# Splitting the last value output over two PSUM banks and two copying engines, with a new order of the segment

## The chip, the cores and the metric

The kernel runs on one core of one Trainium2 chip. The metric is device microseconds (us) of one execution.

## The reference, cut to what matters

Two branches over the same 2048 tokens of width 640 are mixed by a gate. Branch A (sliding-window attention) is untouched. Branch B is the one that changes: 64 segments in a row, each of 8 memory tokens and 32 new tokens, 32 heads of 192, and the memory of a segment is the output of the one before.

```
g = sigmoid((x * gate_w).sum(-1));  out = g * A(x) + (1 - g) * B(x)
# B:
for s in range(64):
    h = concat([mem, x[:, 32*s:32*s+32]])            # 40 tokens x 640
    q, k, v = h @ Wq, h @ Wk, h @ Wv                 # 32 heads x 192
    p = softmax(mask(q @ k.T * 192**-0.5))
    o = (p @ v) @ Wo                                 # 40 x 640
    mem = o[:, :8];  out += [o[:, 8:]]               # the next segment needs mem
```

## The kernel before

A segment is worked off in four groups of eight heads. For each group there are chunks of the projections (q, k, v: 20 matmuls each), turns of q and k (tq, tk), scores (s) with the softmax on VectorE and ScalarE, the turn of p, the value output (pv: 12 matmuls) and the output projection (o: six row tiles of Wo with ten matmuls each, all four groups added up in one PSUM bank). TensorE works in exactly the order of STEP; the other engines are list-scheduled around it.

The weights of branch B do not all fit beside each other. 21 tiles of a segment (11 of 384 KB, 10 of 320 KB) are streamed from HBM again in every segment, through a ring of five slots; STREAMED names them. A load is issued by SyncE when the tile five before it has been used up.

```
RING = 5
STEP = "q0 k0 v0 tk0 tq0 k1 q1 s0 tk1 tq1 q2 s1 tq2 k2 k3 p0 tk2 q3 pv0 v1 s2 p1 o0 tk3 tq3 pv1 v2 s3 p2 o1 pv2 v3 p3 o2 pv3 o3"
STREAMED = {"q": ((), (), (3, 4), (4,)), "k": ((4,), (3, 4), (4,), (4,)), "v": ((), (4,), (4,), (4,)),
            "o": ((1, 3, 5), (2, 5), (2, 5), (1, 3, 5))}
KEPT = {..., "hT": (1, [P, KT, SEG])}               # one buffer for the turned input
...
def values(s, g):                                    # L933, L938
    o = sc.buf("mm")                                 # one PSUM bank for the three blocks
    ... 12 matmuls, block b into columns 160*b ...
    sc.op("ACT", act(480), lambda: nc.scalar.copy(OT, o[:, 0:480]), reads=[o], writes=[OT])
...
def oproj(s, g):                                     # L957
    for c in range(6):                               # row tile c of the group
        for r in range(2):
            i, b = divmod(2 * c + r, 3)              # pair of heads i, block b of OT
            ... 5 matmuls with rhs = OT[:, b, i, :] ...
    if g == 3:
        sc.op("DVE", ..., copy(hT_next[:, :, 0:MEM], ps_o), after=[xl])     # L968: memory of the next segment
...
if chunks % 12 == 0:                                 # after v3
    hts[s + 1] = load_x(s + 1)                       # L745: x part of the next hT, by DMA
```

## Time and profile before

| | kernel before |
|---|---|
| time, median of the first three runs | 2259.32 us (2255.68 to 2266.35) |
| profiled run: span, granted TensorE clock | 2254.3 us, 0.980 |
| first copy of a memory into hT (start of the segments proper) | 567.9 us |
| one segment, mean of 62 | 26.20 us |

### The profile page before, as it was taken

Reading aid. Unit: us, or ns where it says so; the run is one execution under the profiler, and the core shown is the slowest. Engines: PE = TensorE matmul, PEld = TensorE weight load, DVE = VectorE, ACT = ScalarE, POOL = GpSimd, SP = SyncE. Lnnn points to the kernel's source line nnn. Section 1 sums busy time; section 2 is a strip of 40 time slices with the busy share of each in tenths; the row PEclk is TensorE's granted clock in tenths of the full one; section 3 lists DMA queues with packets and bytes.
Section 4 is the critical chain, followed back from the end, with each engine's and each line's share of the span. In section 5 each row is a group of like instructions: output and inputs, shape, how many; then the busy total and the mean of one; then the engine's idle time right before and its main releaser. Section 6 shows DMA issues by size and latency. Waiting matters only on the chain.

```text
span 2254.3 us, 112850 instructions
## 1 busy us (share of the span) xinstructions
PE 2056.8 (91%) x49093; PEld 1497.5 (66%) x49093; DVE 1124.8 (50%) x3942; ACT 1055.2 (47%) x2385; POOL 692.7 (31%) x1999
## 2 busy tenths in 40 slices
PE   7999999998899899999999999999999989999995
PEld 5777777885666666666666666666666666666663
DVE  6988885233444444444444444444444444444444
ACT  4888886223344444444444344444434434444443
POOL 5555554012222222222222222222222222222220
PEclk9999999999999999999999999999999999999996
DMA  3322211677899999999999899989989988999997
GB/s 123 97 74 87 82 46 64 242 276 242 290 311 312 305 300 313 305 313 323 302 312 307 296 305 317 316 296 322 317 294 311 311 290 298 305 312 318 314 314 238
DMA packets 263840, 591.69 MB, mean 262 GB/s; under 512 B 54696, under 2 KB 71344, under 8 KB 263344
## 3 DMA queue, kind: packets, MB, share of 16 engines
q1 hardware_dynamic: 240096, 537.19, 71.4%
q0 software_dynamic: 18976, 43.03, 5.6%
q8 instruction: 384, 6.29, 1.1%
q10 hardware_dynamic: 4272, 4.26, 0.6%
q14 instruction: 112, 0.92, 0.1%
HBM read 554.98 MB, written 36.97 MB: 263 GB/s over the span
## 4 chain that ended last, share of the span: by engine, by line
PE 71%; DMA 19%; ACT 4%; issue 3%; POOL 1%; DVE 1%; SPq 0%; ACTq 0%; DVEq 0%; POOLq 0%
DMA t_w<-w_packed 17%; PE ps_o L957 12%; PE ps_k L787 9%; PE ps_q L787 9%; PE ps_v L787 7%; PE ps_pv L933 4%; PE p_m L282 4%; PE p_s L327 4%; PE t_psum L596 4%; PE tr_q L802 2%; PE t_psum L619 2%; PE tr_k L802 2%; PE p_o L411 2%; PE S_ps L859 2%; ACT t_tok L792 1%
## 5 line engine op out<-in xcount | busy, mean ns | idle before, releaser
L787 PEld LDWEIGHTS <-b_hT 128*32 128x32 bf16 x15360 | 372.1, 97 | 272.4 <-issue 42.4
L957 PE MATMUL ps_o<-t_OT,w_o 128*128 128x40 bf16 x8960 | 328.9, 180 | 60.7 <-ACT t_OT L938 44.5
L957 PEld LDWEIGHTS <-w_o 128*128 128x128 bf16 x8960 | 281.0, 96 | 69.3 <-issue 56.3
L957 PE MATMUL ps_o<-t_OT,t_w 128*128 128x40 bf16 x6400 | 263.8, 180 | 27.4 <-DMA t_w<-w_packed 17.6
L357 DVE CUSTOM_DVE_ANT_0 a_junk<-p_s,a_mask 128x384 bf16<-128x384 f32 (+2 forms) x512 | 253.6, 529 | 42.3 <-PE p_st L327 29.8
L834 POOL COPY t_K<-t_xqk 128x64 bf16<-128x64 bf16 x256 | 60.6, 237 | 679.0 <-PE S_ps L859 675.0
L787 PE MATMUL ps_q<-w_q,b_hT 128*32 128x384 bf16 x4352 | 229.1, 334 | 23.7 <-DVE b_hT L968 22.9
L387 ACT ACTIVATE a_pt<-p_st 128x384 bf16<-128x384 f32 (+2 forms) x512 | 219.9, 474 | 41.7 <-PE p_st L327 34.2
L938 ACT CAST t_OT<-ps_pv 128x480 bf16<-128x480 f32 x256 | 143.2, 559 | 202.6 <-PE ps_pv L933 195.2
L957 PEld LDWEIGHTS <-t_w 128*128 128x128 bf16 x6400 | 206.7, 96 | 38.1 <-DMA t_w<-w_packed 28.1
L787 PE MATMUL ps_v<-w_v,b_hT 128*32 128x384 bf16 x4352 | 226.4, 329 | 1.8 <-issue 1.6
L869 DVE TENSOR_REDUCE sm_mx<-S_ps 128x4 f32<-128x160 f32 x256 | 82.6, 323 | 257.9 <-PE S_ps L859 257.8
L787 PE MATMUL ps_k<-w_k,b_hT 128*32 128x384 bf16 x3840 | 205.3, 332 | 0.0
L792 ACT CAST t_tok<-ps_q 128x384 bf16<-128x384 f32 x256 | 122.7, 479 | 147.1 <-PE ps_q L787 143.1
L825 DVE COPY t_K<-tr_k 128x256 bf16<-128x256 bf16 x256 | 75.2, 294 | 225.3 <-PE tr_k L802 221.4
L395 POOL TENSOR_SCALAR_AFFINE_SELECT a_pt<-a_pt 128x512 bf16<-128x512 bf16 x240 | 147.6, 637 | 125.5 <-ACT a_pt L387 124.5
L916 DVE TENSOR_TENSOR t_PTx<-PT_ps,mk_x 128x320 bf16<-128x320 f32 x256 | 124.6, 487 | 105.3 <-PE PT_ps L909 105.3
L792 ACT CAST t_vtok<-ps_v 128x384 bf16<-128x384 f32 x256 | 122.7, 479 | 112.8 <-PE ps_v L787 112.8
L811 ACT COPY b_QT<-tr_q 128x384 bf16<-128x384 bf16 x256 | 123.0, 480 | 105.5 <-PE tr_q L802 105.5
L792 ACT CAST t_tok<-ps_k 128x384 bf16<-128x384 f32 x256 | 122.7, 479 | 105.4 <-PE ps_k L787 105.3
L757 POOL DMA_DIRECT2D t_xqk<-xbqk x256 | 139.4, 545 | 86.7 <-POOL b_QT L815 38.8
L875 ACT ACTIVATE S_ps<-S_ps 128x160 f32<-128x160 f32 x256 | 74.4, 291 | 155.7 <-DVE S_ps L872 141.3
(151 smaller groups left out, 4100.7 us busy)
## 6 DMA issues: line engine op xcount, KB each, us to landing
t_w<-w_packed SPq DMA_DIRECT2D x714, 384.0 KB, 4.9
t_w<-w_packed SPq DMA_DIRECT2D x640, 320.0 KB, 4.6
t_xqk<-xbqk POOLq DMA_DIRECT2D x256, 48.0 KB, 4.4
xbqk<-t_ts POOLq DMA_DIRECT2D x12, 768.0 KB, 5.4
w_q<-in_B_Wq_dram SPq DMA_DIRECT2D x17, 384.0 KB, 4.8
w_v<-in_B_Wv_dram SPq DMA_DIRECT2D x17, 384.0 KB, 9.1
xbv<-t_ts POOLq DMA_DIRECT2D x16, 384.0 KB, 3.5
t_xv<-xbv POOLq DMA_DIRECT2D x64, 96.0 KB, 4.6
```

The costliest lines, as they stand in the source:

```text
L282: nc.tensor.matmul(view()[:, gg, :], lhsT=Wp[:, kt, 4 * g:4 * g + 4, :].rearrange("p h d -> p (h d)"), rhs=T(k["xT"])[:, kt, :], start=(kt ...
L327: nc.tensor.matmul(T(out)[:, i * P:(i + 1) * P], lhsT=b if keys_first else a, rhs=a if keys_first else b, start=True, stop=True, tile_posi ...
L357: sc.op("DVE", 135 + n / 0.96, lambda: nc.vector.tensor_tensor_reduce(out=T(junk)[:, 0:n], in0=T(s)[:, 0:n], in1=mask[:, NKB * P - n:], op ...
L387: sc.op("ACT", act_ns(n), lambda: nc.scalar.activation(out=T(pt)[:, h % 4, 0:n], in_=T(s)[:, 0:n], func=ACT.Exp), reads=[s], writes=[pt])
L395: nc.gpsimd.affine_select(out=v, in_=v, compare_op=op, fill=0.0, base=0, pattern=[[0, 4], [sign, P]], channel_multiplier=-sign)
L757: sc.op("DMA", 500, lambda: nc.gpsimd.dma_start(tile_of(qk)[:].rearrange("p i b t -> p (i b t)"), xbqk[g, :, s].rearrange("p i c -> p (i c ...
L787: nc.tensor.matmul(t[32 * j:32 * j + 32, 0:384], lhsT=tile_of(hT)[:, kt, :], rhs=w[:, j * 384:(j + 1) * 384], start=(kt == kts[0]), stop=( ...
L792: sc.op("ACT", act(384), lambda: nc.scalar.copy(tile_of(tok)[:], b["tile"][:, 0:384]), reads=[b], writes=[tok])
L811: nc.scalar.copy(dst, tq["tile"][:].rearrange("p b (j t) -> p b j t", t=SEG))
L916: nc.vector.tensor_tensor(out=tile_of(dst)[:], in0=PT["tile"][:, i, :, :].unsqueeze(2).to_broadcast([P, 2, 4, L]), in1=mk.unsqueeze(1).uns ...
L938: sc.op("ACT", act(480), lambda: nc.scalar.copy(tile_of(OT)[:].rearrange("p b j l -> p (b j l)"), o["tile"][:, 0:480]), reads=[o], writes= ...
L957: nc.tensor.matmul(t[:, dt * L:(dt + 1) * L], lhsT=w[:, r * D + dt * P:r * D + (dt + 1) * P], rhs=OT["tile"][:, b, i, :], start=(g == 0 an ...
```

## The change

The intent: at the end of a segment TensorE waits for one ScalarE copy of all three blocks of the last value output. With block 0 in a bank of its own, ScalarE can copy it while TensorE still computes blocks 1 and 2, VectorE copies these, and Wo's row tiles are ordered by block so that the first 20 matmuls of the projection need block 0 alone. The opening of the segment is reordered too, and the streamed tiles are distributed anew.

```diff
-            i, b = divmod(2 * c + r, 3)
+            b, i = divmod(2 * c + r, 4)             # rows of Wo by block; also where Wo is packed
-STEP = "q0 k0 v0 tk0 tq0 k1 q1 s0 tk1 tq1 q2 s1 tq2 k2 k3 p0 tk2 q3 pv0 v1 s2 p1 o0 tk3 tq3 pv1 v2 s3 p2 o1 pv2 v3 p3 o2 pv3 o3"
+STEP = "k0 q0 tk0 q1 tq0 k1 s0 tq1 tk1 k2 q2 s1 p0 tk2 q3 v0 tq2 k3 pv0 v1 s2 p1 o0 tq3 tk3 pv1 v2 s3 p2 o1 pv2 v3 p3 o2 pv3 o3"
-        o = sc.buf("mm")
+        o = [sc.buf("mm")]
+        o.append(sc.buf("mm") if g == 3 else o[0])
 ... (the matmuls in two parts: block 0, blocks 1 and 2)
-        sc.op("ACT", act(480), ... copy(OT, o[:, 0:480]))
+        sc.op("ACT", act(160), ... copy(OTa, o[0][:, 0:160]))
+        if g == 3:
+            sc.op("DVE", dve(320), ... copy(OTb, o[1][:, 160:480]))
+        else:
+            sc.op("ACT", act(320), ... copy(OTb, o[1][:, 160:480]))
 ... (oproj reads OTa for row tiles 0 and 1, OTb for the others)
-STREAMED = {"q": ((), (), (3, 4), (4,)), "k": ((4,), (3, 4), (4,), (4,)), "v": ((), (4,), (4,), (4,)),
-            "o": ((1, 3, 5), (2, 5), (2, 5), (1, 3, 5))}
+STREAMED = {"q": ((4,), (4,), (), (3, 4)), "k": ((), (4,), (3, 4), (4,)), "v": ((), (4,), (4,), (4,)),
+            "o": ((1, 3, 5), (1, 3, 5), (2, 5), (2, 5))}
```

More of the change, by code (lines that the diff above doesn't have):

```diff
@@ L713, in branch_B @@
         "tok": (2, [P, 384]), "vtok": (1, [P, 384]), "K02": (1, [P, 4, 2, L]),
-        "PTm": (1, [P, 2, 4, L]), "PTx": (1, [P, 2, 4, L]), "OT": (1, [P, 3, 4, L]), "Pm": (1, [P, 4, SEG]),
+        "PTm": (1, [P, 2, 4, L]), "PTx": (1, [P, 2, 4, L]), "OTa": (1, [P, 1, 4, L]), "OTb": (1, [P, 2, 4, L]), "Pm": (1, [P, 4, SEG]),
         "xqk": (2, [P, 2, 12, MEM]), "xv": (1, [P, 384]), "oT": (1, [P, KT, SEG]),
@@ L924, in values, with f @@
         V, xv = made.pop(("v", s, g)), tails[s]
-        o = sc.buf("mm")
-        def f():
-            t = tile_of(o, [P, 512], FP32, "ps_pv")
-            for b in range(3):
+        o = [sc.buf("mm")]
+        o.append(sc.buf("mm") if g == 3 else o[0])
+        def f(part):
+            t = tile_of(o[part], [P, 512], FP32, "ps_pv")
+            for b in (1, 2) if part else (0,):
                 for i, (p, v) in enumerate(((PTx, tile_of(xv)), (PTm, V["tile"]))):
@@ L933, in f @@
                         nc.tensor.matmul(t[64 * a:64 * a + 64, 160 * b:160 * b + 160], lhsT=v[:, c:c + 64],
-                                         rhs=p["tile"][:, a, :, :].rearrange("p j l -> p (j l)"), start=(b == 0 and i == 0),
+                                         rhs=p["tile"][:, a, :, :].rearrange("p j l -> p (j l)"), start=(i == 0 and (b == 0 or b == 1 and g == 3)),
                                          stop=(i == 1), tile_position=(0, 64 * a), skip_group_check=True)
-        sc.op("PE", 430, f, reads=[PTm, PTx, V, xv], writes=[o], name=("pv", s, g), mode=64)
-        OT = sc.buf("OT")
-        sc.op("ACT", act(480), lambda: nc.scalar.copy(tile_of(OT)[:].rearrange("p b j l -> p (b j l)"), o["tile"][:, 0:480]),
-              reads=[o], writes=[OT])
+        for part in range(2):
+            sc.op("PE", 143 * (1 + part), lambda part=part: f(part), reads=[PTm, PTx, V, xv], writes=[o[part]], name=("pv", s, g, part), mode=64)
+        OT = [sc.buf("OTa"), sc.buf("OTb")]
+        flat = lambda k: tile_of(OT[k])[:].rearrange("p b j l -> p (b j l)")
+        sc.op("ACT", act(160), lambda: nc.scalar.copy(flat(0), o[0]["tile"][:, 0:160]), reads=[o[0]], writes=[OT[0]])
+        if g == 3:
+            sc.op("DVE", dve(320), lambda: nc.vector.tensor_copy(flat(1), o[1]["tile"][:, 160:480]), reads=[o[1]], writes=[OT[1]])
+        else:
+            sc.op("ACT", act(320), lambda: nc.scalar.copy(flat(1), o[1]["tile"][:, 160:480]), reads=[o[1]], writes=[OT[1]])
         made["O", s, g] = OT
@@ L954, in f @@
             for r in range(2):
-                i, b = divmod(2 * c + r, 3)
+                b, i = divmod(2 * c + r, 4)
                 for dt in range(KT):
                     nc.tensor.matmul(t[:, dt * L:(dt + 1) * L], lhsT=w[:, r * D + dt * P:r * D + (dt + 1) * P],
-                                     rhs=OT["tile"][:, b, i, :], start=(g == 0 and c == 0 and r == 0 and dt == 0),
+                                     rhs=OT[b > 0]["tile"][:, b - (b > 0), i, :], start=(g == 0 and c == 0 and r == 0 and dt == 0),
                                      stop=(g == 3 and c == 5 and r == 1), skip_group_check=True)
         for c in range(6):
-            sc.op("PE", 10 * 25.4, lambda c=c: f(c), reads=[OT] + [wb[c]] * (wb[c] is not None), writes=[o_b], name=("o", s, g, c),
+            sc.op("PE", 10 * 25.4, lambda c=c: f(c), reads=[OT[c > 1]] + [wb[c]] * (wb[c] is not None), writes=[o_b], name=("o", s, g, c),
                   mode=128, after=[loads.get(("o", g, c))])
```

## The prediction

> **What bounds the kernel now.** I began with the slices of the page, to find the stage, then took the busy times of one stretch, then the waits of the matrix engine in it, then single rows of one segment.
>
> ```profile
> PE   7999999998899899999999999999999989999995
> DMA  3322211677899999999999899989989988999997
> ...
> 568.00:2192.00 1624.00, 1487.71 (x39184) 1067.13 (x39184) 730.38 (x2542) 685.91 (x1550) 447.16 (x1426) 0.99 0.92 308
> ...
> PE ps_o L957 <- ACT t_OT L938: 43.8, 62, 0.7
> PE ps_q L787 <- DVE b_hT L968: 22.6, 62, 1.7
> PE ps_o L957 <- issue: 16.4, 22, 1.8
> PE ps_o L957 <- DMA t_w<-w_packed: 15.5, 40, 1.2
> PE tr_q L802 <- ACT t_tok L792: 12.7, 61, 0.2
> ...
> DVE b_hT L968 <- DMA b_hT<-xa_dram: 25.8, 6, 5.0
> ```
>
> The slices show two regimes. The first quarter (sliding-window branch and the projections of the tails) hardly feels this change. From slice 10 on, TensorE and the DMA engines are both at nine tenths: the memory branch, 64 segments in a row, each of which needs the output of the one before. The stretch from 568 to 2192 us (the long row: TensorE 1487.71 of 1624.00 us busy, DMA share 0.92, 308 GB/s) holds exactly 62 of them, so one segment takes 1624 / 62 = 26.2 us. The time follows from what happens within a segment, times 64.
>
> The waits say that TensorE stands still for the value output of the last head group (t_OT, 43.8 / 62 = 0.71 us a segment, every time), for the new memory (b_hT, 0.36), for a token copy (0.20), and for weights that are streamed from HBM. The next rows show the first of these in one segment:
>
> ```profile
> 1220.57 0.24 PE L933 MATMUL ps_pv<-t_PTm,t_vtok 128*64 128x160 bf16 x2
> 1221.51 0.40 PE L957 MATMUL ps_o<-t_OT,w_o 128*128 128x40 bf16 x10 [0.71 <-ACT t_OT L938]
> ...
> 1220.90 0.56 ACT L938 CAST t_OT<-ps_pv 128x480 bf16<-128x480 f32 x1 [2.37 <-PE ps_pv L933]
> 1223.44 0.29 ACT L971 CAST t_oT<-ps_o 128x160 bf16<-128x160 f32 x1 [1.98 <-DVE b_hT L968]
> ...
> 1218.26 0.54 POOL L745 DMA_DIRECT2D b_hT<-xa_dram  x1 [2.40 <-PE PT_ps L909]
> ...
> DMA to landing us min/median/max: 2.8/4.2/5.7
> ```
>
> The last value matmul starts at 1220.57, ScalarE starts its 480-column copy 0.33 us later and takes 0.56, and the output projection starts 0.04 after that: a serial chain in which TensorE has nothing else to do, since this is the end of the segment. The last two rows matter below: the x part of the next segment's hT is fetched when the last v chunk is done, and lands 4.2 us (median) after its issue.
>
> **What the Trainium skill says.** "PSUM — Partial Sum Buffer", section "PSUM bank collisions raise a hardware error", says that a reader must not touch a bank while TensorE writes it. That is why one bank forces the copy to wait for all three blocks, and why the change takes a second bank; the trace agrees as far as it goes (the copy always starts after the last value matmul). "Perfetto Trace Analysis", section "Optimizing Scalar/DVE Operations", advises to break up an instruction that causes bubbles elsewhere on an engine that is not saturated: ScalarE is busy 685.91 of 1624 us and VectorE 730.38, so both have room. "Runtime: NRT & Kernel Launch", section "Instruction fetch mechanics", says instructions come in blocks of 256 over a DMA queue of their own, the cost mostly hidden. The trace agrees on the size (instruction queue: 384 packets, 6.29 MB, so 16.4 KB each, and 2 x 49093 TensorE instructions make 64 bytes each) but not on "hidden": the waits marked "issue" at ps_o come at places a multiple of about 255 TensorE rows apart, up to 1.8 us long. "TensorEngine Tiling (Array Packing)", section "Key Properties", says that a change of tiling mode drains TensorE; here the step between the last matmul of one mode and the first of another is about 0.095 us longer than within a mode (for example 0.149 against 0.056 us from a transpose to a projection chunk).
>
> **The change part by part.** (1) *Two banks, two engines, in group 3.* Block 0 goes to one bank in four matmuls, blocks 1 and 2 to another in eight. ScalarE can start 0.33 us after the second pair of block 0 (1220.29 in the segment above), so at 1220.62; 160 columns take 0.29 us (the t_oT copy has this shape); the projection can start at 1220.62 + 0.29 + 0.04 = 1220.95 instead of 1221.51. Its first 20 matmuls read block 0 alone, since Wo's rows are now ordered by block, and take 20 x 0.025 = 0.50 us, to 1221.45. VectorE starts at 1220.90; I estimate 0.49 us for 320 columns from the 0.48 us of its 320-element PSUM operations, done at 1221.43. It is just in time, so the wait falls by 0.56 us a segment and about 0.15 to 0.2 stays.
>
> (2) *Groups 0 to 2* get two ScalarE copies (0.29 + about 0.43 us) instead of one of 0.56: 3 x 0.16 us more ScalarE a segment. Between value output and projection there lies a v chunk, 0.93 us or more, so nothing waits. Cost on the path: none.
>
> (3) *New order.* I walked through the opening by hand with the durations of the rows (chunk 0.815, scores 0.43, transposes 0.17). The wait of tr_q for the token copy goes, since p0, tk2, q3 and v0 now lie between q2 and tq2: with the lost overlap 0.27 us. But the order has 26 changes of tiling mode instead of 24: 2 x 0.095 = 0.19. The new close spots (tk0 one chunk after k0, s0 one chunk after tq0, p0 right after s1) come out with 0.02 to 0.2 us to spare. Net gain 0.08.
>
> (4) *Which weights are streamed.* As many as before: 11 of 384 KB and 10 of 320 KB a segment, 8.08 MB with the rest. The transfers are no faster, only placed elsewhere: o0 to o3 stream 3, 3, 2, 2 row tiles instead of 3, 2, 2, 3.
>
> PE-side sum: 0.56 + 0.08 = 0.64 us a segment, 64 x 0.64 = 41 us. I do not expect to get it all.
>
> **What takes the place of the wait.** *First, the weight stream.* The ring has five slots; a load is issued when the tile five before it is used up (0.03 to 0.3 us after, by the rows) and lands 4.2 to 5.3 us later on average, depending on the place. So a tile waits where five tiles are used in under about 4.9 us. I measured this span in every segment: the third tile of o0 has 4.43 us at the shortest and costs TensorE 0.21 us on average, the second 4.74 and 0.10, the last of o3 4.17 and 0.12, the last of k1 4.94 and 0.15. With the few others this is about 0.75 us a segment. Laying out the new order with the same durations, the spans in o0 and o3 get longer (5.0 us and more), but o1 gets about 4.6, 4.0, 4.0 and o2 4.1 and 3.7. To bring these up to the 4.5 that the others end at takes about 0.8 us, together about 1.1: 0.35 more than now. Some of it is not new, because the instruction block that stalls around o2 (about 0.4 us a segment of "issue") arrives meanwhile; I count 0.2. There is also the rate itself: 8.08 MB in 25.6 us is 316 GB/s against 308 now; the best single segment had 325 GB/s in 24.49 us, so the floor of the stream is near 24.9 us a segment.
>
> *Second, the load of hT.* For each segment I compared its landing with the end of the last ps_o matmul: in 6 of 62 it came later (the row of 25.8 us above), and in 31 the lead was under 0.5 us. Taking 0.55 us from the time between issue and end raises the mean lateness from 0.07 to 0.23 us: 0.16 is lost, some less if o2 waits for weights in the same interval; I count 0.1.
>
> Sum: 0.64 - 0.2 - 0.1 = 0.34 us a segment, 64 x 0.34 = 22 us; 2259 - 22 = 2237, rounded to 2238.
>
> **Rivals.** (a) *The gain comes through whole.* For it: the t_OT wait is there in all 62 segments and nothing hides it. Against it: DMA at 0.92. Time: 2259 - 41 = 2218. If the more even opening also removes weight waits, a little under 2214. (b) *The stream is the bound.* For it: nine tenths in every slice, and the tight spans in o1 and o2. Against it: loads are mostly issued late because the ring waits for TensorE, so there is some room in the engines. Time: 2250 to 2262, the old time. (c) *hT becomes the end of the segment.* Then the t_OT wait reappears as a longer b_hT wait; time 2245. (d) *A slip in the opening:* scores or p0 waiting in each segment, 0.3 us or more; time 2255 to 2270. My walk speaks against it, with little margin.
>
> **Range and chances.** Runs of one kernel spread by 10 us here, and rivals (a) and (b) bracket the rest: 2210 to 2264. For over 2% faster it must fall under 2214, which needs the full gain and something more: 0.11. Over 2% slower needs 0.7 us a segment of new waits, more than any rival gives: 0.03. Within 2%: 0.86.
>
> **What would show it.** Right: a ps_o wait for the block-0 copy of about 0.15 to 0.2 us a segment instead of 0.71, no wait of the third row tile for VectorE, tr_q's wait gone, t_w waits in o1 and o2 up, a larger share of DMA releases before b_hT. The prediction is wrong if the weight waits fall although the segment got shorter (then the places of the loads matter more than my spans say), or if S_ps or PT_ps shows a new wait.

## More of the kernel before

The slices and waits are read in the prediction. One view it does not show is the chain that ended last, followed back from the last instruction: first the shares of the span by engine, then by instruction group. This is the kernel before:

```profile
PE 71%; DMA 19%; ACT 4%; issue 3%; POOL 1%; DVE 1%; SPq 0%; ACTq 0%; DVEq 0%; POOLq 0%
DMA t_w<-w_packed 17%; PE ps_o L957 12%; PE ps_k L787 9%; PE ps_q L787 9%; PE ps_v L787 7%; PE ps_pv L933 4%; PE p_m L282 4%; PE p_s L327 4%; PE t_psum L596 4%; PE tr_q L802 2%; PE t_psum L619 2%; PE tr_k L802 2%; PE p_o L411 2%; PE S_ps L859 2%; ACT t_tok L792 1%
```

The largest single entry is already the stream of weights (t_w, 17%); the copy of the value output, which the change attacks, is inside "ACT 4%".

## The result, and the profile after

The changed kernel takes 2288.76 us (median of 4 runs, 2280.26 to 2297.33); the kernel before took 2260.49 in the same rounds (4 runs, 2255.68 to 2266.35). The ratio is 1.0124, with a 95% interval from 1.0075 to 1.0173. Ratios and intervals are from fast runs of the same rounds, so not quite the ratio of the medians quoted. The kernel became slower, by about 28 us, and the time lies outside the predicted range.

The slices of the changed kernel (TensorE and the DMA engines, busy tenths in 40 slices):

```profile
PE   7999999998899999999989999899999999999995
DMA  4322211768899999999999999999998999999898
```

The stretch of its 62 segments, 575 to 2218 us (columns: length, busy time and instruction count of TensorE, its weight loads, VectorE, ScalarE and GpSimd, then granted clock, DMA share, GB/s):

```profile
575.00:2218.00 1643.00, 1510.09 (x39184) 1064.83 (x39176) 768.19 (x2603) 676.48 (x1736) 447.13 (x1426) 0.99 0.92 305
```

The picture is the same, only 19 us longer: 1643 us instead of 1624 for the same 62 segments, so 26.5 instead of 26.2 us each, at 305 instead of 308 GB/s. The waits of TensorE in this stretch (columns: total us, times, longest):

```profile
PE ps_o L964 <- DMA t_w<-w_packed: 57.8, 95, 2.6
PE ps_k L787 <- DVE b_hT L975: 45.0, 62, 1.8
PE ps_o L964 <- ACT t_OTa L942: 9.9, 61, 0.2
PE ps_o L964 <- issue: 8.8, 16, 1.0
```

And two waits of VectorE in the same stretch:

```profile
DVE b_hT L975 <- DMA b_hT<-xa_dram: 94.8, 50, 2.8
DVE b_hT L975 <- PE ps_o L964: 16.6, 11, 3.4
```

The wait for the value output fell from 43.8 to 9.9 us, as intended, and tr_q no longer waits for a token copy. But the output projection now waits 57.8 us for streamed weights (15.5 before), and the first chunk of the next segment 45.0 us for hT (22.6 before). The two VectorE rows say why hT is late: in 50 of 61 segments its copy waits for the load of x (6 before).

Rows of one segment of the changed kernel (start, duration, engine, line, operation, count, idle time before and its releaser):

```profile
1227.96 0.40 PE L964 MATMUL ps_o<-t_OTb,w_o 128*128 128x40 bf16 x10
1229.05 0.42 PE L964 MATMUL ps_o<-t_OTb,t_w 128*128 128x40 bf16 x10 [0.69 <-DMA t_w<-w_packed]
...
1235.58 0.23 PE L935 MATMUL ps_pv<-t_PTm,t_vtok 128*64 128x160 bf16 x2
1235.98 0.66 PE L964 MATMUL ps_o<-t_OTa,w_o 128*128 128x40 bf16 x20 [0.16 <-ACT t_OTa L942]
...
1237.93 1.00 PE L787 MATMUL ps_k<-w_k,b_hT 128*32 128x384 bf16 x20 [0.29 <-DVE b_hT L975]
```

The last three rows are the split at work: from the last value matmul to the projection it takes 0.40 us here, where the rows of before had 0.94, and the remaining row tiles follow without a wait for VectorE. The first two rows are what went wrong, in o1: its third streamed tile is not there yet.

The chain that ended last, in the changed kernel:

```profile
PE 64%; DMA 22%; issue 8%; POOL 3%; ACT 2%; DVE 1%; SPq 0%; POOLq 0%; DVEq 0%; ACTq 0%
DMA b_hT<-xa_dram 10%; PE ps_q L787 10%; PE ps_k L787 10%; DMA t_w<-w_packed 9%; PE ps_v L787 6%; PE ps_o L964 5%; PE p_m L282 4%; PE p_s L327 4%; PE t_psum L596 4%; PE ps_pv L935 3%; PE tr_q L802 2%; PE tr_k L802 2%; PE S_ps L859 2%; PE S_ps L852 2%; PE p_o L411 2%
```

The load of hT's x part, which was not among the entries of before, now leads the list with 10%: where it is the last to arrive, the chain runs through it and not through the matmuls and weights beside it.

**Where the time went.** I summed the rows in two ways. First, TensorE's waits of over 0.15 us by what ended them, in us per segment (mean of 62 segments of the profiled run, from one hT copy to the next):

| per segment, us | value copy | token copy | weights | hT | issue | segment |
|---|---|---|---|---|---|---|
| before | 0.71 | 0.21 | 0.44 | 0.37 | 0.41 | 26.20 |
| changed | 0.16 | 0.01 | 0.96 | 0.73 | 0.23 | 26.51 |

The removed waits (0.55 and 0.20) came back as 0.52 for weights and 0.36 for hT, less 0.18 for issue: the waits together came out level (2.14 before, 2.09 after). What the segment is longer by is time in which TensorE counts as busy, 1510.09 instead of 1487.71 us for the same matmuls in the two stretches above, 0.36 us a segment. Of this, 0.19 are the two more changes of tiling mode that the prediction booked, and about 0.11 is an estimate for the clock (13.6 us more of half clock, at half speed); part of the wait in o1 is booked as busy, too (at full clock its matmuls count 1.84 instead of 1.62 us), while other groups got a little shorter.

Second, for the segments that ran wholly at full clock I took the shortest time that each of the 36 groups of TensorE work ever took, start to start, and summed them: that is the segment without accidents. It fell from 24.41 to 23.83 us, by 0.58. The mean above that rose from 1.53 to 2.30 us, by 0.77; 0.88 of the 2.30 lie in o1 and 0.59 in o3 with the start of the next segment. So at full clock a segment is 0.19 us longer, 62 x 0.19 = 12 us. The other 7 or 8 us of the 19.5 that the segments lost come from stretches at half clock: 44 us in 13 of them, against 31 us in 7 (not counting one of 10 us at the start of each). The rest of the 24.3 us between the profiled runs lies outside: 6.6 us ahead of the first hT copy (half of it in branch A, which is the same code and had more half-clock time in that run), less 1.7 us at the end.

### The profile page after: what moved, and what is told of

Read it like the earlier page. It is cut to its first block, busy times and chain, and to the rows that moved or that the text cites. A ratio compares the mean times of both kernels' runs of the same rounds, so it can differ in the third digit from the quotient of the medians.

```text
span 2278.6 us, 113297 instructions
## 1 busy us (share of the span) xinstructions
PE 2084.5 (91%) x49093; PEld 1497.6 (66%) x49093; DVE 1164.2 (51%) x4006; ACT 1045.4 (46%) x2577; POOL 692.5 (30%) x1999
## 4 chain that ended last, share of the span: by engine, by line
PE 64%; DMA 22%; issue 8%; POOL 3%; ACT 2%; DVE 1%; SPq 0%; POOLq 0%; DVEq 0%; ACTq 0%
DMA b_hT<-xa_dram 10%; PE ps_q L787 10%; PE ps_k L787 10%; DMA t_w<-w_packed 9%; PE ps_v L787 6%; PE ps_o L964 5%; PE p_m L282 4%; PE p_s L327 4%; PE t_psum L596 4%; PE ps_pv L935 3%; PE tr_q L802 2%; PE tr_k L802 2%; PE S_ps L859 2%; PE S_ps L852 2%; PE p_o L411 2%
## 5 line engine op out<-in xcount | busy, mean ns | idle before, releaser
L787 PEld LDWEIGHTS <-b_hT 128*32 128x32 bf16 x15360 | 364.5, 97 | 277.7 <-DVE b_hT L975 52.0
L964 PE MATMUL ps_o<-t_OTb,t_w 128*128 128x40 bf16 x5120 | 211.5, 180 | 66.8 <-DMA t_w<-w_packed 60.1
L787 PE MATMUL ps_k<-w_k,b_hT 128*32 128x384 bf16 x4096 | 219.2, 335 | 45.9 <-DVE b_hT L975 45.3
L787 PE MATMUL ps_q<-w_q,b_hT 128*32 128x384 bf16 x4096 | 218.6, 334 | 0.1
L964 PE MATMUL ps_o<-t_OTb,w_o 128*128 128x40 bf16 x5120 | 189.7, 179 | 5.4 <-issue 3.4
L964 PE MATMUL ps_o<-t_OTa,w_o 128*128 128x40 bf16 x3840 | 138.8, 180 | 12.0 <-ACT t_OTa L942 10.2
L327 PE MATMUL p_s<-a_k,a_q 64*128 64x128 bf16 x1440 | 146.6, 220 | 0.7 <-issue 0.7
L327 PE MATMUL p_st<-a_qa,a_k 64*128 64x128 bf16 x1440 | 143.2, 219 | 3.8 <-ACT a_pt L387 2.4
```

The lines of the kernel that those rows point to most:

```text
L327: nc.tensor.matmul(T(out)[:, i * P:(i + 1) * P], lhsT=b if keys_first else a, rhs=a if keys_first else b, start=True, stop=True, tile_posi ...
L787: nc.tensor.matmul(t[32 * j:32 * j + 32, 0:384], lhsT=tile_of(hT)[:, kt, :], rhs=w[:, j * 384:(j + 1) * 384], start=(kt == kts[0]), stop=( ...
L964: nc.tensor.matmul(t[:, dt * L:(dt + 1) * L], lhsT=w[:, r * D + dt * P:r * D + (dt + 1) * P], rhs=OT[b > 0]["tile"][:, b - (b > 0), i, :], ...
```

## The experiments

Theory A: the gain of the split is real, and it is lost because three streamed tiles in o1 come too close together (the wait for weights) and the load of hT has too little time (the wait for hT); undo both and the gain appears. Theory B: TensorE's waits are only where the DMA side shows; the segment runs at the pace at which streamed weights come, and what is removed in one place returns in another. Later a third suspect joined, the blocks of instructions that are fetched through the same DMA engines.

All results agreed with the reference, also those that use wrong weights (e5 to e8): the comparison is not tight enough to see a few of Wo's row tiles exchanged.

| run | median us | before, same rounds | ratio [95%] | us per segment |
|---|---|---|---|---|
| e1: changed, old plan for Wo | 2262.99 | 2265.40 | 0.9999 [0.9976, 1.0022] | 26.21 |
| e2: changed, two hT buffers | 2267.19 | 2265.40 | 1.0007 [0.9987, 1.0026] | 26.25 |
| e3: both | 2261.48 | 2265.40 | 0.9980 [0.9963, 0.9996] | 26.23 |
| e4: before with the split alone | 2260.67 | 2265.40 | 0.9983 [0.9929, 1.0036] | 26.09 |
| e5: before, three tiles less streamed | 2172.50 | 2259.12 | 0.9635 [0.9606, 0.9663] | 24.93 |
| e6: e3, three tiles less streamed | 2159.96 | 2259.12 | 0.9581 [0.9548, 0.9614] | 24.62 |
| e7: before, six slots | 2288.67 | 2259.12 | 1.0141 [1.0101, 1.0181] | 26.13 |
| e8: e1, six slots | 2286.68 | 2259.12 | 1.0134 [1.0103, 1.0164] | 26.03 |
| e9: before with new order and plan, no split | 2301.12 | 2265.29 | 1.0160 [1.0111, 1.0209] | 26.81 |
| e10: before, blocks pinned early | 2240.78 | 2265.29 | 0.9906 [0.9870, 0.9943] | 25.97 |
| e11: before, blocks pinned in o2 | 2283.94 | 2265.29 | 1.0085 [1.0053, 1.0117] | 26.51 |
| e12: e13 with pinned blocks | 2222.38 | 2265.29 | 0.9812 [0.9773, 0.9851] | 25.61 |
| e13: before with split and two hT | 2247.24 | 2262.68 | 0.9908 [0.9880, 0.9936] | 26.09 |
| e14: e3 with pinned blocks | 2249.84 | 2262.68 | 0.9961 [0.9937, 0.9984] | 26.07 |
| e15: changed, pinned blocks | 2282.81 | 2262.68 | 1.0080 [1.0053, 1.0107] | 26.55 |
| e16: e13 with another pinned place | 2224.72 | 2262.68 | 0.9814 [0.9769, 0.9859] | 25.67 |

The last column is from the profiled run of each kernel, 62 segments.

### First set: undo the parts (e1 to e4)

**e1**, the changed kernel with the distribution of Wo's streamed tiles of before (three in o3, two in o1):

```diff
-            "o": ((1, 3, 5), (1, 3, 5), (2, 5), (2, 5))}
+            "o": ((1, 3, 5), (2, 5), (2, 5), (1, 3, 5))}
```

> The changed kernel with one thing undone: the row tiles of Wo that are streamed in o0, o1, o2, o3 are 1,3,5 / 2,5 / 2,5 / 1,3,5 again, as before, instead of 1,3,5 / 1,3,5 / 2,5 / 2,5. New order, split value output and the new streaming of q and k stay. Theory A (the third streamed tile of o1 is used too soon after the tile five places before it, and costs 0.8 us a segment; the whole of o1 takes 2.57 us instead of 1.63): o1 falls back to about 1.65 us, some waits return in o3 (0.1 to 0.2 us), the wait of the first k chunk for hT falls a little or stays near 0.7 us; the segment shortens by 0.5 to 0.8 us, the whole by 30 to 50 us: 2240 to 2260. Theory B (the new order as such is at fault, through hT's late landing and the DMA rate of 308 GB/s): the weight waits only move to another place and the time stays within 10 us of the changed kernel's 2289.

**e2**, the changed kernel with two buffers for hT, so that the load of x need not wait until the segment's last v chunk has read the old one:

```diff
-"hT": (1, [P, KT, SEG])
+"hT": (2, [P, KT, SEG])
```

> The changed kernel with two hT buffers instead of one, so that the x part of the next segment is fetched a whole segment earlier, and the copy of the new memory never waits for its landing. Theory A (hT's landing costs 0.73 - 0.29 = 0.44 us a segment on the path, beside the waits in o1): b_hT waits fall to 0.29 us a segment, landing never ends the wait of L975, the weights' ring gets its slots a little sooner, and of 0.44 x 64 = 28 us about half to all comes through: 2262 to 2276. Theory B (the weight stream binds alone, and whatever is gained at hT is lost again at o1's third tile): under 8 us, 2281 or more, with o1 growing from 2.57 us by about as much as hT's wait falls.

**e3**, both edits.

> Both: the changed kernel with the old plan of Wo's streamed tiles and two hT buffers. Theory A (two separate losses hide a real gain of about 0.8 us a segment on the matrix engine's side): 2215 to 2235, faster than the kernel before by 1 to 2%; the segment at 25.3 to 25.6 us. Theory B (the stream's rate is the floor, whatever the order): not under 2250, DMA share above 0.93 in all stretches.

**e4**, the kernel before with the split and Wo's rows by block, but with the STEP and STREAMED of before.

> The kernel before with only the first part of the change: value output of the last group in two banks copied by two engines, Wo's row tiles ordered by block; old order, old streaming plan. Theory A: the wait of o3 for the value output falls from 0.71 to about 0.17 us a segment as it did in the changed kernel, but the b_hT wait rises from 0.36 to 0.6 or more because the landing does not move; a gain of 0.2 to 0.4 us a segment, 2235 to 2250. If the split itself is what hurts (extra instructions on ScalarE and VectorE, another PSUM buffer of three held), 2265 or more.

Measured: waits of TensorE in the 62 segments of e1:

```profile
PE ps_o L964 <- issue: 22.5, 33, 1.7
PE ps_k L787 <- DVE b_hT L975: 21.2, 62, 1.7
PE ps_o L964 <- DMA t_w<-w_packed: 18.7, 44, 1.7
```

The same of e2:

```profile
PE ps_o L964 <- DMA t_w<-w_packed: 62.1, 81, 2.8
PE ps_k L787 <- DVE b_hT L975: 18.1, 62, 0.3
```

e1 takes the 28 us back: ratio 0.9999 where the changed kernel had 1.0124. The wait for weights at ps_o falls from 57.8 to 18.7 us and, without hT being touched, its wait falls from 45.0 to 21.2: hT now lands after the last ps_o matmul in 5 segments instead of 51, because the third tile of o3 holds up the segment's end instead. e2 shows the mirror image. With hT ready early its wait shrinks to 18.1 us, never over 0.3 (that is the copy itself), the time is back at that of before (1.0007), and the wait for weights grows. So either remedy alone removes the loss. Both together (e3) are worth no more than one: 0.998. Theory A expected 2240 to 2260 us for e1 (missed by 3 us), 2262 to 2276 for e2 (met), 2215 to 2235 for e3 and 2235 to 2250 for e4; the last two missed, though e4's four runs split (two near 2249, two near 2272), so that its ratio is the least certain. In e4 the value copy's wait is 0.16 us a segment, and the weights' wait has risen from 0.44 to 0.61. In all four, 26.1 to 26.25 us per segment remain, as before the change. Theory B looks better.

### Second set: what sets the pace (e5 to e8)

**e5** leaves out three of the 21 streamed tiles, all of Wo (12% of a segment's bytes), and uses a neighbouring resident tile in their place, a wrong result. **e6** does the same to e3's kernel.

```diff
+ALIAS = {("o", 0, 3): ("o", 0, 2), ("o", 1, 5): ("o", 1, 4), ("o", 2, 5): ("o", 2, 4)}
-        return weights.tiles[u] if b is None else b["tile"]
+        return weights.tiles[ALIAS.get(u, u)] if b is None else b["tile"]
 ... (and these three neither streamed nor resident)
```

> Wrong result on purpose: the kernel before, in which three of the ten streamed row tiles of Wo (the fourth of o0, the last of o1 and of o2) are not loaded; the matmuls read a resident neighbour instead. The same instructions on TensorE, 12% fewer streamed bytes. Theory A (the weight stream sets the length of a segment, 26.2 us, in the kernel before as well): the segment falls to what TensorE and its fixed waits need, 24.8 to 25.2 us, the whole to about 2180 to 2200; the rate of the DMA falls below 300 GB/s and the waits for t_w under 0.2 us a segment. Theory B (the waits for weights are local, from too short a distance between single tiles): only the waits at the dropped tiles go, 0.2 to 0.4 us a segment, 2235 to 2250.

> Wrong result on purpose: the same three tiles dropped from the kernel of e3 (split value output, new order, old plan of Wo's tiles, two hT buffers). Theory A (the gain of 0.6 to 0.8 us a segment on TensorE's side is real and is hidden by the stream alone): 24.2 to 24.5 us a segment, 35 to 50 us faster than the same cut of the kernel before (e5). Theory B (the gain was never there, something else in the new order costs as much): within 15 us of e5.

**e7** and **e8** give the ring six slots instead of five, e7 in the kernel before, e8 in e1's. The sixth slot did not fit; for its room one resident tile of Wo is replaced by its neighbour (wrong) and the stage ahead of branch B has one staging buffer instead of two, which makes that part some 40 us longer. The segments must therefore be compared, not the whole times.

```diff
-RING = 5
+RING = 6
-        shape = {"ts": (2, [P, P // MEM, 2, 12, MEM])}
+        shape = {"ts": (1, [P, P // MEM, 2, 12, MEM])}
+ALIAS = {("o", 3, 2): ("o", 3, 0)}
```

> The kernel before with six slots in the ring of streamed weights instead of five. For the space, one resident row tile of Wo is replaced by its neighbour (wrong result on purpose, no change to the stream) and the tails' projections have one staging buffer instead of two, which lengthens only the part ahead of the segments. Theory A (the rate of the DMA, about 309 GB/s over a segment, is the bound): the segment stays at 25.9 to 26.2 us, rate not over 313 GB/s, loads only take longer (5.5 us instead of 4.8). Theory B (the depth of the ring is the bound: tiles are issued too late): segment at 25.2 to 25.6 us, rate 317 to 322 GB/s, waits for t_w down by more than half.

> The same six slots in the kernel of e1 (changed kernel with the old plan of Wo's tiles, one hT buffer). Theory A: as e1, 26.0 to 26.2 us a segment. Theory B: 24.9 to 25.3 us a segment, that is 0.3 us or more under e7, as the split value output then shows.

Measured: the stretch of the 62 segments of e5 (columns as for the stretch above):

```profile
566.00:2111.00 1545.00, 1454.33 (x39184) 1051.92 (x39180) 725.33 (x2541) 685.51 (x1550) 447.53 (x1426) 1.00 0.87 285
```

And that of e6:

```profile
567.00:2093.00 1526.00, 1475.71 (x39174) 1048.14 (x39175) 762.44 (x2603) 678.68 (x1736) 446.97 (x1425) 1.00 0.88 288
```

Twelve per cent less to stream makes a segment 1.27 us shorter (26.20 to 24.93) though TensorE does the same matmuls and still waits 0.71 us for the value copy. Its waits for weights fall to 0.06 us, for issue to 0.11. The times were 2172.5 us against the 2180 to 2200 of theory A, and 24.93 us a segment within its 24.8 to 25.2. Here e6, with the split, is shorter, but by 0.31 us a segment, not by the 0.54 of the split's mechanism; in time 12.5 us, as theory B had it (within 15), where A had expected 35 to 50. The rows say where the rest went: e6's waits are 0.67 us a segment shorter than e5's, but TensorE is busy 0.34 us longer for the same matmuls (1475.71 against 1454.33 us). So the new order costs TensorE time even with a light stream. One would read e5 as "the stream's bytes set the pace"; e12 below shows that this is too simple. Also, with three tiles less, five slots reach over more work, so e5 by itself does not separate the bytes from the spans; e7 is meant for that.

The waits of TensorE in the segments of e7:

```profile
PE ps_o L957 <- ACT t_OT L938: 45.0, 62, 1.0
PE ps_o L957 <- issue: 33.0, 33, 2.6
```

With a sixth slot the waits for weights vanish (0.44 to 0.02 us a segment), and a segment gets no shorter to speak of: 26.13 against 26.20, since the waits marked "issue" double from 0.41 to 0.88 us. In e8 they are 1.24, with 0.03 for weights. Both segments are as theory A expected (25.9 to 26.2, and 26.0 to 26.2 for e8). So the depth of the ring is not what limits, and the issue waits are not a constant of the kernel: in these two, with more loads in flight, TensorE stands longer with no instruction. Both theories were silent on that.

### Third set: the new order, and the instruction blocks (e9 to e12)

The issue waits have a place. The kernel before has 1268 TensorE instructions a segment (632 matmuls, as many weight loads, 4 semaphore instructions), and 1268 = 5 x 256 - 12: a boundary of blocks of 256 moves by 12 instructions from one segment to the next. Of the 36 issue waits before matmuls in its 62 segments, 34 lie at exactly the same offset from such a moving grid, the other two one instruction beside it. The packets of the instruction queue in the trace say the same: there is one of 16 KB for each of 384 blocks, and each of the 36 waits ends 1.27 to 1.62 us after the end of its block's packet, although these packets come only every 5 us or so (1.16 to 1.75 us for all issue waits of e7, e8, e10 and e11). So they are the arrival of instruction blocks. Adding 12 tiny instructions to a segment makes it 1280 = 5 x 256, and the boundaries then stay at five fixed places, which a single larger pad in the first segment chooses.

**e9**, the kernel before with the STEP and STREAMED of the changed one, but the value output in one bank, copied by ScalarE at once.

> The kernel before with the new order and the new streaming plan, but the value output of the last group undivided (one bank, one copy) and Wo's row tiles in the old order within a group. Theory A (the DMA side sets the pace, and a fixed wait of TensorE taken away only makes room for another): as slow as the changed kernel, 26.4 to 26.6 us a segment, 2275 to 2300, with fewer waits for hT and weights and the 0.71 us for the value output back. Theory B (waits add up): the changed kernel plus 0.55 us a segment, 2310 to 2330.

**e10** and **e11**, the kernel before with 12 instructions more (6 matmuls of one column into an unused column of ps_o, with their weight loads) in each segment, and 42 or 178 more once: e10 has boundaries 104 instructions (and 360, 616, 872, 1128) before the segment's end, e11 240 before it, which is inside o2.

```diff
+        def pad(n):
+            t = tile_of(o_b, [P, 512], FP32, "ps_o")
+            for _ in range(n):
+                nc.tensor.matmul(t[:, 500:501], lhsT=ident[:], rhs=ident[:, 0:1], start=False, stop=True, skip_group_check=True)
+        if g == 3:
+            sc.op("PE", 150, lambda n=6 + (21 if s == 0 else 0): pad(n), writes=[o_b], name=("pad", s, g), mode=128)   # e11: 89
```

> The kernel before with 12 more TensorE instructions in each segment (six weight loads and six one-column matmuls into unused columns of the output bank, ahead of the last output projection, where TensorE waits 0.7 us anyhow) and 42 more, once, in the first segment. By the trace a segment has 1268 instructions, 12 less than five blocks of 256, so the places at which the 'issue' waits come wander through the segment; with 1280 they stand still, here about 104 instructions ahead of the segment's end, where the kernel before shows hardly any. Theory A (these waits are for instruction blocks that come over the same DMA engines, and they are part of what the segment pays): issue waits fall from 0.41 to under 0.15 us a segment, segment 25.5 to 25.8 us, 2220 to 2240. Theory B (the byte rate alone is the bound): the waits for weights take over, 26.0 to 26.2 us, 2255 to 2265.

> As e10, but 136 instructions further back: the block ends stand still about 240 instructions ahead of the segment's end, in o2, where the trace of the kernel before has the most of these waits. Theory A: an issue wait at the same place of nearly every segment, 0.6 to 1.2 us each, segment 26.4 to 26.8 us, 2270 to 2300. Theory B: within 10 us of the kernel before, and the place of the waits does not matter.

**e12**, the old order and plan with the split, two hT buffers, and the pad (47 in the first segment: boundaries 156 before the end and every 256 earlier).

> Candidate for a kernel faster than both: order and plan of the kernel before, divided value output, two hT buffers, and the block ends pinned about 156 instructions ahead of the segment's end, where e4 had its shortest segments (25.4 us). Theory A: 25.1 to 25.5 us a segment, 2195 to 2225. Theory B: 26.0 us, 2250 to 2260, as e4.

Measured: waits of TensorE in the 62 segments of e9:

```profile
PE ps_o L957 <- DMA t_w<-w_packed: 61.5, 91, 2.1
PE ps_k L787 <- DVE b_hT L968: 30.7, 62, 1.7
```

The waits at ps_o in e10:

```profile
PE ps_o L957 <- DMA t_w<-w_packed: 20.6, 48, 1.6
PE ps_o L957 <- issue: 3.9, 10, 1.1
```

The same in e11:

```profile
PE ps_o L957 <- issue: 32.1, 38, 2.1
PE ps_o L957 <- DMA t_w<-w_packed: 6.1, 16, 1.0
```

And a row of e11's weight loads (start, duration, operation, count, idle time before) at the pinned place in o2, where the projection stands for 0.49 us with no instruction to work on:

```profile
1207.70 0.11 PEld L957 LDWEIGHTS <-w_o 128*128 128x128 bf16 x2 [0.49 <-issue]
```

e9 is slower than everything else: the new order with its plan costs by itself (ratio 1.016), the weights' wait is all there without the split, and adding the split to it, which gives the changed kernel, takes 0.30 us off a segment. The split never was the culprit. Its time lies just above theory A's range (2275 to 2300) and below B's (2310 to 2330), so about half of the 0.55 us is kept here and neither theory fits.

e10 and e11 compute the same and differ in where five block boundaries lie. They are 43 us apart (2240.78 and 2283.94 us in the same rounds). In e11 TensorE waits for instructions at exactly the pinned place, 240 before the end, in 38 of 62 segments, 32.1 us in all; e10's places cost little. Not all of the 43 us need be the waiting itself: the mean granted clock was 0.981 in e10's nine runs and 0.972 in e11's eight, and 0.009 of 2260 us is about 20 us, an estimate of what stretches at half clock can account for. In the profiled runs, half clock touches 6 segments of e10 and 22 of e11, and the others are only 0.08 us apart (25.84 and 25.92). Whether these stretches follow from the longer waits is not shown. That a block's place is worth more than the whole intended gain was in nobody's plan.

e12 is the fastest kernel, with e16 below not to be told from it: 2222.38 us, 0.9812 of before (the interval reaches over the 2% line), at 315 GB/s over the segments, more than the 308 of before at a higher DMA share (0.93 against 0.92). So the bare byte rate was no ceiling either. Its two largest waits are

```profile
PE ps_q L787 <- DVE b_hT L981: 18.1, 62, 0.3
PE ps_pv L935 <- issue: 14.6, 22, 1.4
```

of which the first is the floor of the hT copy (0.29 us a segment), and the second is again an instruction block, where it was pinned.

### Fourth set: taking e12 apart (e13 to e16)

**e13** is e12 without the pad. **e14** is e3 (new order, old plan for Wo, two hT) with a pad of 5 matmuls a segment (its segment has 1270 instructions) and 22 once, boundaries at 104. **e15** is the changed kernel itself with that pad. **e16** is e12 with 21 instead of 47 once, boundaries at 104.

> e12 without the additional instructions: old order and plan, divided value output, two hT buffers, block ends wandering. Theory A (the place of the block ends is worth what e10 against the kernel before shows, about 0.25 us a segment or more): 2240 to 2258. Theory B (two hT buffers brought e12's gain): 2215 to 2230.

> The kernel of e3 (divided value output, new order, old plan of Wo's tiles, two hT buffers) with its block ends pinned 104 instructions ahead of the segment's end. Its segment has 1270 instructions by the trace, two more than the old order, so 10 are added here and 44 once. Theory A (what hid the gain in e3 were the blocks): 2215 to 2235, issue waits from 0.65 to under 0.3 us a segment. Theory B (the new order itself has weight waits that take the place): 2245 or more.

> The changed kernel as it is, with the same 10 and 44 additional instructions. Theory A (its loss is the wait of o1's third tile and hT's late landing, the blocks have little part in it: 0.23 us of issue waits a segment): 2275 to 2290, o1 still at 2.4 us or more. Theory B (the blocks' places make the difference between the two kernels): 2245 to 2260.

> e12 with the block ends 104 instead of 156 instructions ahead of the segment's end. In e12 there were 24 issue waits at 156 and 23 at 1177 of the 62 segments, in e10 at 104 almost none. Theory A (it goes by the place): issue waits fall from 0.46 to under 0.25 us a segment, 2205 to 2220. Theory B (without the 0.71 us wait for the value output any place is as bad): 2220 to 2230.

Measured: e13 is at 0.9908, so split and two hT buffers together are worth 0.9% in the old order; pinning is worth about as much again (0.9906 alone in e10, 0.9812 and 0.9814 with both): the two add up. e15 stays slow, at 1.008, with waits of 0.93 us for weights and 0.59 for hT: the loss of the changed kernel is not one of unlucky blocks. e14 reaches 0.9961; against e16, the same pinned place in the old order, the new order still costs 25 us. e16 has fewer issue waits than e12 (0.15 against 0.46 us a segment) and more for weights (0.62 against 0.33), and the same time: I had expected 2205 to 2220 (theory A) and it missed by 5 us; theory B's 2220 to 2230 fits. For e13 and e15 theory A's ranges were met, for e14 theory B's. Below some level, then, even the blocks trade with the weights.

## Why the prediction was wrong

Going through its own steps:

1. *Two banks, two engines in group 3.* Right, in mechanism and size. It promised 0.56 us; the shortest time from pv3 to o3 fell from 1.31 to 0.77 us, by 0.54. About 0.16 us of the wait stays (0.15 to 0.2 promised), and no row tile waits for VectorE. The row pair shown above is this step.
2. *Groups 0 to 2: cost on the path none.* Right: no wait for their copies appears.
3. *New order: net gain 0.08.* Right as far as TensorE's own path goes: tr_q's wait went (0.21 to 0.01), the path from s1 to tq2 shortened by the 0.27 that the prediction names, and the new close spots hold (S_ps and PT_ps have no wait to speak of, 0.3 us in the whole run). The sum of shortest times fell by 0.58 where steps 1 to 3 promised 0.64.
4. *What takes the place of the wait.* This failed, in two terms. "To bring these up to the 4.5 that the others end at takes about 0.8 us, together about 1.1: 0.35 more than now ... I count 0.2": measured, weights rose by 0.52. "I count 0.1" for hT: measured 0.36. Together 0.88 in place of 0.30, of which 0.18 came back in the waits for issue. That is the larger part of the 0.65 us between the 0.34 promised and the 0.31 lost; the rest is TensorE's busy time, 0.36 longer where step 3 booked 0.19, and 0.75 of waits removed where steps 1 and 3 had 0.83. What came is nearest to rival (b) plus rival (c), both at once; I had bracketed each alone, and the result lies above both.

Why the weight term was mis-sized can be named. The spans that I had laid out for o1 were right: 4.6, 4.0 and 4.0 us, measured 4.61, 4.01 and 4.15 at the shortest. Wrong was the landing time: I let every tight span settle at the 4.5 us at which other tiles of the old kernel stood. The first two tiles of o1 landed about 4.2 us after issue, the third after 5.12; TensorE waited for it in 49 of 61 segments, and its span was stretched to 5.22 on average. The step to its first matmul took 0.79 us on average (0.025 when nothing is late), and o1 as a whole takes 2.57 us where it took 1.63. One number for all places of a stream was the error, and the trace of the kernel before could have told: the load in the same place of the ring, issued 0.6 us after the one before it when o0's second streamed tile is used up, took 5.3 us there as well, and 5.4 in e1. In these two kernels it is v3's tile (384 KB; the next load, of 320 KB, took 5.3 and 5.6 us), with a span of 5.5 us or more; the new plan put a tile with 4.15 there. Over the whole segment of the kernel before, the nine loads issued within 0.9 us of their predecessor landed after 5.2 us on average, the other twelve after 4.6 (from 4.2 to 6.0 by place, where the prediction has 4.2 to 5.3). The old plan has the same crowding in o3, where it lies across the segment's end and partly beside the waits there; e1 shows that moving the third tile back takes away the entire 28 us.

Why hT was mis-sized: I took 0.55 us off its lead and raised its mean lateness from 0.07 to 0.23. It landed late in 51 segments instead of the 6 of before, and 4.51 us (median) after its issue instead of 4.23. As I read it, the time that o1 loses does not help it: the load is issued when v3 is done, after o1, so o1's wait lies ahead of it, and o3, which used to be held up by its own third tile, no longer gives it time. That would be why e1 (third tile back in o3) cures the hT wait too: o3 takes 2.08 us there from its first matmul to its last, 1.79 in the changed kernel.

The larger error is above both: the prediction treated TensorE's waits as costs that can be removed one by one and priced a replacement of 0.3 us. In e1, e3 and e4, where the two mis-sized terms are mended, the segment is still 26.1 to 26.2 us, and almost none of the 0.54 us is left. The runs point to the DMA side as what sets the pace: less to stream (e5), 1.27 us a segment; more slots (e7), the same pace with another name on the wait; instruction blocks in another place (e10, e11), 43 us. "Loads are mostly issued late because the ring waits for TensorE, so there is some room in the engines", the argument against rival (b), was not enough: e7 issues them earlier and gains nothing.

How blocks and weights hinder each other is shown only in part. In the kernel before, the packet of an instruction block took 0.97 us (median) whether its block came late or not; for the 36 late blocks it started 2.8 us (median) after the block boundary before, for the others 1.7. So the fetch was late, not long. What held its start back no run shows. The Trainium skill, "DMA: Bandwidth & Descriptors", section "Queues, rings and completion order", says that each DMA engine takes packets from its queues in turn and switches only between packets; a 16 KB block could thus hold up a weight packet (2.2 KB on average) behind it by up to its own length. That is argued, not shown, and does not explain a block that starts late.

One part of the 28 us needs an account of its own: half-clock stretches, 44 us instead of 31 within the segments of the profiled runs, worth about 7 us. In the two traces each follows waits of TensorE that add up to 1.1 to 2.6 us within the 8 us before it, so I take them for a consequence of longer waits; but a fifth to a quarter of all moments in these stretches follow waits as long, so such waits are not enough by themselves. Counted with the one at the start, e5 and e6, with hardly a wait for weights, have two such stretches each, e12 four, the kernel before eight, the changed one fourteen; but e1, with a segment as short as before, has twelve, and e7 seventeen. That is a rough correlation, not an experiment, and the cause stays open.

**Left open:** why a load issued close behind another lands later; what delays the fetch of an instruction block; why the new order, with plan and blocks mended (e14), remains 25 us behind the old one (e16); what limits the DMA side at a share of 0.92 to 0.93 and 305 to 315 GB/s, since neither slots nor bytes alone do.

## What to carry to other kernels

When TensorE and the DMA engines are both at nine tenths, as here, do not price a TensorE wait that is removed at its full length: take some of the stream away first and see what the gain becomes. Compare waits and busy time both, since here the waits came out level and the segment still grew. Measure the landing time of loads by their place in the stream, not as one number. Look at where the deadlines of streamed tiles lie, not only at how many there are, since three close together cost 28 us here and giving a late load a second buffer cured the same loss. And when a repeated body has a fixed number of instructions, look whether its issue waits sit on a grid of blocks: 12 padding instructions gave as much as the whole repaired change, and both together the fastest version, 2222 us, 1.9% under the kernel before.

## What the Trainium skill lacked or had wrong

- "Runtime: NRT & Kernel Launch", "Instruction fetch mechanics": the page calls the cost of crossing a block boundary "mostly hidden". With busy DMA engines it is not: 0.41 us a segment of issue waits in the kernel before, up to 1.24 in e8, and 43 us between e10 and e11, which differ only in where the boundaries lie. TensorE goes on 1.27 to 1.62 us after the packet of the block has ended (kernel before). The block size of 256 instructions agrees: the waits come at exactly that grid.
- "DMA: Bandwidth & Descriptors", "Queues, rings and completion order": the page has the turn-taking of queues, but nothing on instruction blocks delayed by a stream of loads, or the other way round; with six slots in flight the issue waits doubled, 0.41 to 0.88 us a segment. It also has no landing time for loads of 320 to 384 KB with several in flight: 4.2 us for the first two of o1, 5.1 for the third, 4.2 to 6.0 by place in the kernel before.
- "TensorE: Matmul & The Clock Gate", "Part 1: The HAM clock gate (the "warmup" mystery)": the page lets the clock fall to half after an idle window of about 3.4 us; it also tells of a kernel in which frequent short idle times did it, without a length. The stretches here last 3.41 us or a multiple of it, which agrees, but within the segments they follow waits that add up to only 1.1 to 2.6 us in the 8 us before them, in a TensorE that is busy nine tenths of the time; the longest single gap within the segments of the changed kernel was 2.6 us, and they have thirteen such stretches.
- "TensorEngine Tiling (Array Packing)", "Key Properties": says that a change of mode drains TensorE, without a cost. The step from one mode to another is about 0.095 us longer here than within a mode, 24 times a segment before and 26 after.
